# Scan features read in place by TensorE instead of being moved into one tile per group

## The chip, the core and the metric

The kernel runs on one core of a Trainium2 chip. Its time is the device time of one execution, in microseconds (us). Three runs of the kernel before gave 675.22, 677.21 and 671.78 us, a median of 675.22. The execution that was profiled took 673.33 us, with a span of 671.6 us.

## The reference

The reference has three parts that follow each other. A gated linear scan runs for 4 batches and 8 heads over 768 steps, with a complex decay per step and per feature:

```
S_re, S_im = ar*S_re - ai*S_im + k[t] (x) v[t],  ar*S_im + ai*S_re     # 48 x 48 per head
y[t] = q[t] @ S_re
```

Its outputs, 3072 tokens of 8 x 48 = 384 numbers, go through a mixture of eight experts (tokens with a positive skip score are routed to the expert with the largest logit, relu(x w1) w2, added to x), and then through a second mixture (normalised tokens against normalised expert vectors, every token routed). Everything is float32.

## The kernel before, in words

**Features.** The scan is computed in closed form. The cumulative sums of log magnitude and of phase are taken along time (`front` and `back` in `feat`), and q and k are multiplied by the growth and decay factors and by cosine and sine of the phase. A score between two steps is then a plain dot product over 96 features of a head: 48 "real" products (times cosine) and 48 "imaginary" ones (times sine). The work is cut into 8 groups g (4 batches, two halves of 384 steps); group 0 and group 7 are cut once more in time (`PARTS`). In a group, 384 features of the 8 heads lie on 3 blocks of 128 partitions. VectorE (DVE) writes the real products into tile PR (one buffer) and the imaginary ones over QK (three buffers); both are made at line 536.

**The move.** The 128 partitions of PR and QK don't hold a head's 96 features together. Line 548 moves them by DMA into ST (two buffers), where each head has rows 0 to 95: five transfers per part from PR on SP's queue, five from QK on POOL's queue. `PIECES` lists them, `head` and `row` say where they land.

**Chunks.** A group has 3 chunks of 128 steps, 24 in all (k). For a chunk, TensorE (PE) does the following, with ScalarE (ACT) and DVE emptying PSUM:

- W, line 601: 8 matmuls of 96 rows, one a head, k-features against q-features, into PS0 and PS1 (`half(0)` and `half(1)`); DVE multiplies by the causal mask into WM (line 604).
- K, line 612: 8 transposes of the k-features into PS2 and PS3, copied by ACT to KT (line 615); not for the last chunk of a batch.
- y, line 628: 8 matmuls WM x V and, from the second chunk of a batch on, 8 matmuls with the running state SS, in pairs: the even head's 48 output columns go to PSUM partitions 0 to 47, the odd head's to 64 to 111, all in PS4.
- U, line 637: 8 matmuls KT x V that add to the state in PS5, copied by ACT to SS (line 641); not for the last chunk of a batch.
- x, line 648: 4 matmuls that bring y to token order with the first router's logits; ACT copies the token rows (line 651) and they are stored; DVE reduces the logits (line 654).

After the last chunk the routing is finished, and the two mixtures of experts (lines 938 to 1284) run on PE.

**What sets the order.** All instructions are collected in a list by `Plan`, each with an engine, a cost in us, what it reads and writes, and a due time; `Plan.order` sorts them in a list schedule, forwards and backwards several times, and keeps the shortest. Each engine then executes its own list strictly in that order. Where the planner sees PE idle, `run` inserts filler matmuls (`warm`, line 438) with no use but to keep PE busy. So a change of a cost or of a dependence moves instructions on every engine.

Of the kernel before, what the change touches and what calls it, by code (L numbers as in the profile page):

```python
# [41 lines left out]
FILL = 0.6  # L42
PARTS = {0: ((0, 1), (1, 3)), 7: ((0, 2), (2, 3))}
# [235 lines left out]
def kernel(  # L279
# [132 lines left out]
    NRI, NQK = 4, 3  # L412
    ST = [st_p.tile([P, 2 * H * TS], F32, name=f"ST{i}") for i in range(2)]
    SS = [st_p.tile([96, H, 64], F32, name=f"SS{i}") for i in range(2)]
    WM = [[st_p.tile([P, 4, P], F32, name=f"WM{i}{j}") for j in range(2)] for i in range(2)]
    KT = [[st_p.tile([P, 4, 96], F32, name=f"KT{i}{j}") for j in range(2)] for i in range(2)]
# [4 lines left out]
    QK = [el.tile([P, 2 * NB * TS], F32, name=f"QK{i}") for i in range(NQK)]  # L421
    T1 = [el.tile([P, NB * TS], F32, name=f"T1{i}") for i in range(2)]
    T2 = [el.tile([P, NB * TS], F32, name=f"T2{i}") for i in range(2)]
    PR = el.tile([P, 2 * NB * TS], F32, name="PR")
# [5 lines left out]
    nc.vector.memset(PS[4], 0.0)  # L430
    nc.gpsimd.memset(SQ2, 1.0)
# [8 lines left out]
    def feat(g):  # L440
# [26 lines left out]
        k1, k2, kp = (lambda j: K("t1", g % 2, j)), (lambda j: K("t2", g % 2, j)), (lambda j: K("pr", 0, j))  # L467
# [45 lines left out]
        def back(i, j):  # L513
# [26 lines left out]
            vp = part(PR, 2 * NB, j)  # L540
            dve(2 * n, lambda: mul(vp, vre), kre(j) + kqk(j), kp(j))
            dve(2 * n, lambda: mul(vc, vim), kim(j), kqk(j))
            d = part(ST[g % 2], 2 * H, j)
            for x, ks, a0 in ((vp, kp, 0), (vc, kqk, 1)):
                for y, (h, bk, p0, o, m) in enumerate(PIECES):
                    nh = h[1] - h[0]
                    eng, add, us = (nc.gpsimd, pool, 1.0) if a0 and g in POOLST else (nc.sync, dma, 0.64)
                    add(MOVE * wide(j) / P * nh * m / D, lambda x=x, a0=a0, h=h, nh=nh, bk=bk, p0=p0, o=o, m=m, eng=eng: eng.dma_start(  # L548
                        d[row(h, a0) + o : row(h, a0) + o + m, 2 * h[0] * w : 2 * h[1] * w],
                        x[p0 : p0 + m, 2 * bk * w : 2 * (bk + nh) * w]),  # L550
                        ks(j), [("st", g % 2, y, a0, i) for i in range(j.start, j.stop)], cost=us)

        def run(part):
            plan.bias = LEAD
# [17 lines left out]
    def kst(g, hs, cs):  # L572
        return [("st", g % 2, y, a, i) for y, (h, *_) in enumerate(PIECES)
                if any(h[0] <= x < h[1] for x in hs) for a in range(2) for i in cs]
# [6 lines left out]
    def chunk(k):  # L581
# [3 lines left out]

        def st(z, h):
            o = (2 * H * s0 + head(z, h) * (s1 - s0) + c - s0) * P
            return ST[g % 2][0:96, o : o + P]

# [5 lines left out]
        def half(hh):  # L595
            hs = range(4 * hh, 4 * hh + 4)
            wt = PS[hh][:, 0:512].rearrange("p (h t) -> p h t", h=4)

            def w_():
                for h in hs:  # L600
                    nc.tensor.matmul(wt[:, h % 4, :], lhsT=st(1, h), rhs=st(0, h), start=True, stop=True)  # L601

            pe(0.95, w_, kst(g, hs, [c]), [("ps", hh)], D0 - 4)
            dve(512, lambda: nc.vector.tensor_tensor(  # L604
                WM[k % 2][hh], wt, maskT.rearrange("p (o t) -> p o t", o=1).to_broadcast([P, 4, P]), op=ALU.mult),
                [("ps", hh), "mask"], [("wm", k % 2, hh)], D0 - 2)
            if not last:
                kt = PS[2 + hh][:, 0:384].rearrange("p (h t) -> p h t", h=4)

                def k_():  # L610
                    for h in hs:
                        nc.tensor.transpose(kt[:, h % 4, :], st(1, h), ident[0:96, 0:96])

                pe(0.35, k_, kst(g, hs, [c]), [("ps", 2 + hh)], D0 - 3)
                act(384, lambda: nc.scalar.copy(KT[k % 2][hh], kt), [("ps", 2 + hh)], [("kt", k % 2, hh)], D0 - 1)

        for hh in range(2):
            half(hh)
# [3 lines left out]
        def y_():  # L622
            for p in range(NPR):
                for x in range(2 if i else 1):
                    for j in range(2):
                        h = 2 * p + j
                        w, r = (so[:, h, 0:D], st(0, h)) if x else (vt[:, c, h, :], WM[k % 2][h // 4][:, h % 4, :])
                        nc.tensor.matmul(py[64 * j : 64 * j + D, p, :], lhsT=w, rhs=r, start=(x == 0), stop=(x == 1 or i == 0))  # L628

        pe(1.8 if i else 0.95, y_, [("wm", k % 2, 0), ("wm", k % 2, 1), ("v", g % 2)] + kst(g, range(H), [c])  # L630
           + ([("S", k % 2)] if i else []), [("ps", 4)], D0)
        if not last:
            pu = PS[5][0:96, 0:DM].rearrange("d (h e) -> d h e", h=H)

            def u_():
                for h in range(H):
                    nc.tensor.matmul(
                        pu[:, h, :], lhsT=KT[k % 2][h // 4][:, h % 4, :], rhs=vt[:, c, h, :], start=not i and not h, stop=True, skip_group_check=True)

            pe(1.48, u_, [("kt", k % 2, 0), ("kt", k % 2, 1), ("v", g % 2)], [("ps", 5)], D0 + 1)  # L640
            act(DM, lambda: nc.scalar.copy(sn[:, :, 0:D], pu), [("ps", 5)], [("S", (k + 1) % 2)], D0 + 3)
# [202 lines left out]
    pe(0.5, lambda: nc.tensor.matmul(PS[7][:, 384:512], lhsT=PR[:, 0:P], rhs=ident, start=True, stop=True), [("pr", 0, 0)], [], -100.0)  # L844
# [27 lines left out]
    def make_l():  # L872
# [751 lines left out]
```

## Time and profile before

| | |
|---|---|
| median of three runs | 675.22 us (671.78 to 677.21) |
| the profiled execution | 673.33 us, span 671.6 us |
| PE busy | 606.9 us, 90% of the span |
| DVE busy | 462.1 us, 69% |
| ACT busy | 411.1 us, 61% |
| POOL busy | 187.2 us, 28% |
| DMA | 116.39 MB |

Shares over the whole span mix three stages: the start, in which PE has nothing to do; the scan with its 24 chunks; and the experts. The rows further down are cut by stage. Between two rows of a timeline the difference of their start times says how long the first one held its engine; the duration beside it includes the latency of the last instruction.

### The profile page before, as it was taken

The page shows a single profiled execution, that of the slowest core. Times are in us where ns is not written, and L with a number is a line of the kernel's source. Part 1 is how long each engine was busy: PE and PEld are TensorE (multiplying, and loading weights), DVE is VectorE, ACT ScalarE, POOL GpSimd, SP SyncE. Part 2 cuts the span into 40 slices and gives each one's busy share as a digit, 9 for nine tenths or more (in the row PEclk, how much of TensorE's full clock was granted, in tenths as well). Part 3 has the DMA queues.
Part 4 walks back from the last instruction along what each step waited for, and adds up shares of the span by engine and source line. Part 5 has one row for each costly group of instructions (what it writes and reads, how often), then busy time and mean ns, then how long its engine had stood idle before and what let it go on. Part 6 is the DMA issues. An engine that isn't in the chain of part 4 may idle for free. (4 is left out here: it accounts for less than half of the span.)

```text
span 671.6 us, 12986 instructions
## 1 busy us (share of the span) xinstructions
PE 606.9 (90%) x4764; PEld 581.9 (87%) x4764; DVE 462.1 (69%) x1035; ACT 411.1 (61%) x735; POOL 187.2 (28%) x233
## 2 busy tenths in 40 slices
PE   0179699998999999999999999999999999999993
PEld 0178699987989988999999999989998989999993
DVE  4999699998996465767776657778466474655340
ACT  5997869787887453755555545166467474664430
POOL 5112011014634433223443133233141313213111
PEclk9997889999999999999999999999999999999998
DMA  8748999889476677766644430474325434355101
GB/s 317 277 120 208 202 246 303 239 205 267 114 186 155 227 256 227 252 228 219 194 172 132 129 113 20 113 282 146 118 73 184 153 122 144 129 189 176 47 11 36
DMA packets 39079, 116.39 MB, mean 173 GB/s; under 512 B 8573, under 2 KB 14275, under 8 KB 36322
## 3 DMA queue, kind: packets, MB, share of 16 engines
q1 hardware_dynamic: 28354, 84.97, 40.0%
q0 software_dynamic: 10656, 30.53, 16.4%
q8 instruction: 39, 0.64, 0.4%
q14 instruction: 30, 0.25, 0.1%
HBM read 83.78 MB, written 14.09 MB: 146 GB/s over the span
## 5 line engine op out<-in xcount | busy, mean ns | idle before, releaser
L969 PE MATMUL PS<-x,w 128*128 128x256 f32 (+4 forms) x1152 | 179.3, 313 | 1.1 <-DVE h L982 0.6
L1019 PE MATMUL PS<-w,h 128*128 128x384 f32 x968 | 179.4, 340 | 0.4 <-ACT xA L1278 0.4
L969 PEld LDWEIGHTS PS<-x,w 128*128 128x128 f32 x1152 | 171.4, 190 | 2.7 <-DVE x L945 0.7
L1019 PEld LDWEIGHTS PS<-w,h 128*128 128x128 f32 x968 | 166.1, 189 | 2.2 <-ACT xA L1278 1.7
L975 ACT ACTIVATE h<-PS 128x256 fp32r<-128x256 f32 (+4 forms) x136 | 57.4, 422 | 103.7 <-PE PS L969 103.5
L982 DVE SCALAR_TENSOR_TENSOR h<-PS,h 128x256 fp32r<-128x256 f32 (+3 forms) x152 | 64.7, 436 | 71.3 <-ACT h L975 43.0
L1284 POOL DMA_INDIRECT out<-o,ts2i x30 | 30.9, 1029 | 164.0 <-ACT o L1274 108.9
L919 DVE TENSOR_TENSOR w<-r,w 128x768 fp32r<-128x768 f32 x64 | 59.3, 952 | 8.0 <-ACT w L918 4.4
L913 DVE TENSOR_TENSOR w<-r,w 128x1024 fp32r<-128x1024 f32 x45 | 53.9, 1223 | 11.1 <-ACT w L912 9.9
L601 PE MATMUL PS<-ST 96*128 96x128 f32 x384 | 54.5, 289 | 7.1 <-DVE WM L604 2.9
L601 PEld LDWEIGHTS PS<-ST 96*128 96x128 f32 x384 | 48.4, 199 | 10.1 <-DVE WM L604 3.8
L918 ACT CAST w<-r 128x768 fp32r<-128x768 f32 x64 | 51.7, 834 | 8.9 <-PE PS L1019 6.1
L438 PE MATMUL PS<-cst 128*128 128x128 f32 x332 | 49.2, 295 | 3.3 <-DVE w8s L731 2.2
L912 ACT CAST w<-r 128x1024 fp32r<-128x1024 f32 x45 | 45.7, 1049 | 7.4 <-DMA r<-in_w1b 7.0
L438 PEld LDWEIGHTS PS<-cst 128*128 128x128 f32 x332 | 44.6, 207 | 4.3 <-DVE w8s L731 2.6
L548 POOL DMA_DIRECT2D ST<-QK x50 | 25.6, 524 | 80.7 <-DVE QK L536 37.0
L604 DVE TENSOR_TENSOR WM<-PS,cst 128x512 f32<-128x512 f32 x48 | 32.4, 680 | 14.5 <-PE PS L601 14.4
L944 ACT CAST x<-PS 128x256 fp32r<-128x256 f32 (+4 forms) x48 | 19.8, 426 | 32.4 <-PE PS L938 31.8
L1086 POOL DMA_INDIRECT xd<-o,ts1i x16 | 17.0, 1061 | 78.9 <-DVE o L1083 37.9
L740 POOL DMA_INDIRECT tab<-LG,ixa x24 | 28.7, 1195 | 32.0 <-DMA ts1f<-tab 8.2
L628 PE MATMUL PS<-WM,VT 128*48 128x128 f32 x384 | 37.2, 282 | 0.1
L1032 POOL DMA_INDIRECT xg<-xd,ts2i x30 | 32.0, 1067 | 13.5 <-issue 5.3
(217 smaller groups left out, 982.5 us busy)
## 6 DMA issues: line engine op xcount, KB each, us to landing
r<-in_w1a SPq DMA_DIRECT2D x24, 512.0 KB, 5.7
r<-in_w2a SPq DMA_DIRECT2D x32, 384.0 KB, 3.8
r<-in_w1b SPq DMA_DIRECT2D x24, 512.0 KB, 3.9
r<-in_w2b SPq DMA_DIRECT2D x32, 384.0 KB, 5.4
RI<-in_ri SPq DMA_DIRECT2D x6, 1152.0 KB
QK<-in_qk SPq DMA_DIRECT2D x6, 1152.0 KB, 18.1
ST<-PR SPq DMA_DIRECT2D x12, 432.0 KB, 6.2
ST<-QK POOLq DMA_DIRECT2D x12, 432.0 KB, 10.1
```

Source lines behind the costliest of these rows:

```text
L438: nc.tensor.matmul(PS[7][:, 384:512], lhsT=ident, rhs=ident, start=True, stop=True)
L601: nc.tensor.matmul(wt[:, h % 4, :], lhsT=st(1, h), rhs=st(0, h), start=True, stop=True)
L604: dve(512, lambda: nc.vector.tensor_tensor(WM[k % 2][hh], wt, maskT.rearrange("p (o t) -> p o t", o=1).to_broadcast([P, 4, P]), op=ALU.mul ...
L628: nc.tensor.matmul(py[64 * j : 64 * j + D, p, :], lhsT=w, rhs=r, start=(x == 0), stop=(x == 1 or i == 0))
L912: act(F, lambda s=s: nc.scalar.copy(T["w1"][q % 2][0][s], T["r1"][q % 2][s]), [("r1", q % 2, j), "L"], [k + (0,)])
L913: dve(F, lambda s=s: nc.vector.tensor_tensor(T["w1"][q % 2][1][s], T["r1"][q % 2][s], T["w1"][q % 2][0][s].bitcast(F32), op=ALU.subtract), ...
L918: act(2 * DM, lambda s=s: nc.scalar.copy(T["w2"][0][s], T["r2"][s]), [("r2", j)], [k + (0,)])
L919: dve(2 * DM, lambda s=s: nc.vector.tensor_tensor(T["w2"][1][s], T["r2"][s], T["w2"][0][s].bitcast(F32), op=ALU.subtract), [("r2", j), k + ...
L969: nc.tensor.matmul(ph, lhsT=l, rhs=r, start=(i == 0), stop=(i == len(seq) - 1))
L975: act(wa, lambda f=f, ph=ph: nc.scalar.activation(T[name][:, f, o0 : o0 + wa], ph[:, 0:wa], AF.Relu), [("ps", f % 3), "w" if name == "hA" ...
L982: dve(b - a, lambda f=f, ph=ph, a=a, b=b, o=o: nc.vector.scalar_tensor_tensor(T[name][:, f, o : o + b - a], ph[:, a - c0 : b - c0], 0.0, T ...
L1019: nc.tensor.matmul(po if n == P else po[0 : 2 * stride], lhsT=x, rhs=w[:, f, :], start=(f == 0 and i == 0), stop=(f == NF - 1 and i == len ...
```

## The change

The features are laid out so that heads 0 to 5 lie two to a block, each on 48 partitions that start at 0 or at 64, and PE reads them where DVE wrote them: 48 rows of real products in PR, 48 of imaginary ones in QK, so that a head's dot product is two matmuls of 48 rows added in PSUM. An even head uses the partitions from 0, an odd head those from 64 (two row groups of the array). Heads 6 and 7 fill the gaps (16 rows in each of three blocks) and are still moved to ST, which now holds these two heads alone: six transfers per part from PR and six from QK, of 16 partitions each. PR gets three buffers, QK four. W, K, y and U are rewritten for this; WM and KT are now kept by even and odd heads or by real and imaginary products. PS5 is cleared at the start, and group 0 is given an earlier due time (`LEADS`). The planner's costs for W, K, y and U are named numbers.

```
-PIECES = [((0, 3), 0, 0, 0, 48), ((3, 6), 0, 48, 0, 48), ((6, 8), 0, 96, 0, 32), ...]
+LEADS = {0: -40.0}
+COST_W, COST_K, COST_Y, COST_U = 1.95, 0.36, 2.4, 1.45
+PIECES = [((h, h + 1), h // 2, 64 * (h % 2), 0, 48) for h in range(6)]
+MOVED = [((h, h + 1), b, 48 + 64 * (h - 6), 16 * b, 16) for h in (6, 7) for b in range(NB)]
+PIECES += MOVED
...
-    NRI, NQK = 4, 3
-    ST = [st_p.tile([P, 2 * H * TS], F32, name=f"ST{i}") for i in range(2)]
+    NRI, NQK, NPB = 4, 4, 3
+    ST = [st_p.tile([P, 4 * TS], F32, name=f"ST{i}") for i in range(2)]
...
+    nc.vector.memset(PS[5][:, 0:DM], 0.0)
...
-            pe(0.95, w_, kst(g, hs, [c]), [("ps", hh)], D0 - 4)          # twice, one for 4 heads
+        def w_():
+            for b in range(NB):
+                for a in range(2):
+                    for j in range(2):
+                        nc.tensor.matmul(wt[j][:, b, :], lhsT=xf(1, a, b)[rows(j)], rhs=xf(0, a, b)[rows(j)], start=(a == 0), stop=(a == 1))
+            for j in range(2):
+                nc.tensor.matmul(wt[j][:, NB, :], lhsT=st(1, 6 + j), rhs=st(0, 6 + j), start=True, stop=True)
+        pe(COST_W, w_, sum(kf, []), [("ps", 0), ("ps", 1)], D0 - 4)
...
+                def k_(hh=hh, kt=kt):
+                    for b in range(NB):
+                        nc.tensor.transpose(kt[:, 2 * b : 2 * b + 2, :].rearrange("p h t -> p (h t)"), xf(1, hh, b), ident)
+                    nc.tensor.transpose(kt[:, 6:8, 0:D], st(1, 6 + hh), ident[0:96, 0:96])
...
+            for h in range(H):
+                mm(h, vt[:, c, h, :], WM[k % 2][h % 2][:, h // 2, :], h < 2, not i)
+            if i:
+                for h in (6, 7):
+                    mm(h, so[0:96, h, 0:D], st(0, h), False, True)
+                for b in range(NB):
+                    for a in range(2):
+                        for j in range(2):
+                            mm(2 * b + j, so[rows(j), 2 * b + a, 0:D], xf(0, a, b)[rows(j)], False, a == 1)
...
+                for b in range(NB):
+                    for a in range(2):
+                        for j in range(2):
+                            nc.tensor.matmul(
+                                pu[rows(j), 2 * b + a, :], lhsT=KT[k % 2][a][:, 2 * b + j, :], rhs=vt[:, c, 2 * b + j, :],
+                                start=not i and not a and not b, stop=True, skip_group_check=True)
```

The order of instructions, at three places. In these rows L601 and L606 are W (the L608 rows its last two matmuls), L612 and L620/L621 are K, L628 and L631 are y, L637 and L652/L656 are U, L648 and L668 are x, L438 and L433 are fillers; the numbers behind a tile's name tell its buffer.

First, PE at y of the second chunk of a batch. Before:

```order
L628 MATMUL PS4_101<-WM10_111,VT0_117 48x128 x2
L628 MATMUL PS4_101<-ST0_105,SS1_108 48x128 x2
L628 MATMUL PS4_101<-WM10_111,VT0_117 48x128 x2
L628 MATMUL PS4_101<-ST0_105,SS1_108 48x128 x2
L628 MATMUL PS4_101<-WM11_112,VT0_117 48x128 x2
L628 MATMUL PS4_101<-ST0_105,SS1_108 48x128 x2
```

With the change, the end of the same step and the start of the next chunk's W:

```order
L631 MATMUL PS4_101<-ST0_105,SS1_108 48x128 x2
L631 MATMUL PS4_101<-PR0_135,SS1_108 48x128 x2
L631 MATMUL PS4_101<-QK0_127,SS1_108 48x128 x2
L631 MATMUL PS4_101<-PR0_135,SS1_108 48x128 x2
L631 MATMUL PS4_101<-QK0_127,SS1_108 48x128 x2
L631 MATMUL PS4_101<-PR0_135,SS1_108 48x128 x2
L631 MATMUL PS4_101<-QK0_127,SS1_108 48x128 x2
L606 MATMUL PS0_97<-PR0_135 128x128
L606 MATMUL PS1_98<-PR0_135 128x128
L606 MATMUL PS0_97<-QK0_127 128x128
L606 MATMUL PS1_98<-QK0_127 128x128
```

The state part of y was four pairs that read ST; it is now one pair from ST and six pairs that read PR and QK, and W alternates between the two row groups and between two PSUM banks.

Second, SP's queue at the move of group 2 (the third group). Before:

```order
L653 DMA xd_63<-XT0_119 128x384
L548 DMA ST0_105<-PR_134 48x2304 x2
L548 DMA ST0_105<-PR_134 32x1536
L548 DMA ST0_105<-PR_134 16x768 x2
L653 DMA xd_63<-XT1_120 128x384
```

With the change:

```order
L673 DMA xd_63<-XT0_119 128x384
L465 DMA RI1_124<-in_ri 128x2304
L542 DMA ST0_105<-PR2_137 16x768 x6
L673 DMA xd_63<-XT1_120 128x384
L673 DMA xd_63<-XT0_119 128x384
```

Two transfers of 48 partitions, one of 32 and two of 16 have become six of 16 partitions, and a load of a later group's input stands ahead of them.

Third, PE where the seventh chunk (the first of group 2) begins. Before:

```order
L628 MATMUL PS4_101<-ST1_106,SS0_107 48x128 x2
L648 MATMUL PS6_103<-lane_73,XTT1_122 128x113 x4
L601 MATMUL PS0_97<-ST0_105 128x128 x4
L628 MATMUL PS4_101<-WM10_111,VT1_118 48x128 x2
L628 MATMUL PS4_101<-ST1_106,SS1_108 48x128 x2
```

With the change:

```order
L631 MATMUL PS4_101<-QK1_128,SS1_108 48x128 x2
L433 MATMUL PS7_104<-cst_66 128x128 x4
L668 MATMUL PS6_103<-lane_73,XTT1_122 128x113 x4
L433 MATMUL PS7_104<-cst_66 128x128 x15
L606 MATMUL PS0_97<-PR2_137 128x128
L606 MATMUL PS1_98<-PR2_137 128x128
```

Before, W of the seventh chunk comes ahead of y of the sixth. Now the six chunks of the first batch are done with x and all, 19 fillers stand there, and from here to the end of the scan the order holds 2 more fillers (20 stood behind this place before).

## Rows read from the trace of the kernel before

**Rows 1.** Four stages: length, busy us (x instructions) of each engine, granted clock, DMA share, GB/s.

```profile
39.80:104.93 65.13, 53.60 (x497) 50.82 (x495) 57.13 (x72) 53.16 (x62) 8.01 (x16) 0.84 0.81 196
104.93:237.00 132.07, 125.23 (x1434) 117.85 (x1432) 111.99 (x205) 103.54 (x152) 44.49 (x57) 1.00 0.78 212
237.00:244.70 7.70, 6.46 (x54) 5.87 (x53) 5.50 (x39) 3.74 (x8) 1.10 (x1) 1.00 0.75 221
244.70:671.60 426.90, 412.12 (x2721) 397.83 (x2719) 257.25 (x669) 219.34 (x477) 122.28 (x131) 0.99 0.44 146
```

**Rows 2.** The fillers (L438) alone, third stage: length, PE busy, PEld busy.

```profile
104.93:237.00 132.07, 6.47 (x41) 5.26 (x41) 1.00 0.78 212
```

**Rows 3.** Waits of PE in the third stage: us, times, longest us.

```profile
PE PS L601 <- DVE WM L604: 2.2, 2, 1.7
PE PS L648 <- DVE LG L654: 2.0, 2, 1.2
```

**Rows 4.** Timeline of DVE: start, us, instruction, idle before it.

```profile
60.76 2.53 DVE L536 TENSOR_TENSOR QK<-QK,RI 128x2304 f32<-128x2304 f32 x1
...
83.11 0.69 DVE L604 TENSOR_TENSOR WM<-PS,cst 128x512 f32<-128x512 f32 x1 [5.33 <-PE PS L601]
83.72 1.01 DVE L478 TENSOR_TENSOR_SCAN T<-T,lend,lmt 128x384 f32<-128x384 f32 x1
84.64 2.53 DVE L536 TENSOR_TENSOR PR<-QK,RI 128x2304 f32<-128x2304 f32 x1
...
87.21 2.56 DVE L536 TENSOR_TENSOR QK<-QK,RI 128x2304 f32<-128x2304 f32 x1
...
212.98 0.96 DVE L536 TENSOR_TENSOR QK<-QK,RI 128x768 f32<-128x768 f32 x1
```

**Rows 5.** Timeline of PE: first product, fourth chunk, seventh chunk's W.

```profile
30.29 0.80 PE L844 MATMUL PS<-cst,PR 128*128 128x128 f32 x2 [30.29 <-DVE PR L536]
...
82.27 0.80 PE L601 MATMUL PS<-ST 96*128 96x128 f32 x2 [2.10 <-DMA ST<-QK]
...
104.93 1.07 PE L601 MATMUL PS<-ST 96*128 96x128 f32 x8
```

**Rows 6.** Moves issued up to 104.93 us: count, KB each, median us to landing.

```profile
ST<-QK POOLq DMA_DIRECT2D x4, 432.0 KB, 16.5
```

**Rows 7.** Small moves, up to 240 us: count, KB each, median us to landing.

```profile
ST<-PR SPq DMA_DIRECT2D x4, 16.0 KB, 2.3
ST<-QK POOLq DMA_DIRECT2D x4, 16.0 KB, 3.8
```

**Rows 8.** Timeline of SP: one load that is now issued before the features' inputs.

```profile
5.03 0.92 SPq L798 DMA_DIRECT2D lane<-in_wr  x1
```

**Rows 9.** Timeline of PE in the middle of the scan, at full granted clock.

```profile
132.22 2.04 PE L601 MATMUL PS<-ST 96*128 96x128 f32 x16
134.09 0.49 PE L612 MATMUL PS<-cst,ST 96*128 96x96 f32 x4
134.51 0.43 PE L628 MATMUL PS<-WM,VT 128*48 128x128 f32 x4
134.77 0.39 PE L628 MATMUL PS<-ST,SS 96*48 96x128 f32 x4
...
136.09 0.39 PE L628 MATMUL PS<-ST,SS 96*48 96x128 f32 x4
136.41 1.16 PE L601 MATMUL PS<-ST 96*128 96x128 f32 x8
137.41 1.48 PE L637 MATMUL PS<-VT,KT 128*96 128x48 f32 x16
138.73 1.11 PE L648 MATMUL PS<-lane,XTT 128*128 128x113 f32 x8
```

**Rows 10.** Timeline of PE: three transposes of 128 x 128 in the experts.

```profile
290.30 0.49 PE L1095 MATMUL PS<-cst,o 128*128 128x128 f32 x3
290.54 3.48 PE L969 MATMUL PS<-x,w 128*128 128x256 f32 x27
```

More of the change, by code (lines that the diff above doesn't have):

```diff
@@ L420 @@
     RI = [el.tile([P, 2 * NB * TS], F32, name=f"RI{i}") for i in range(NRI)]
-    QK = [el.tile([P, 2 * NB * TS], F32, name=f"QK{i}") for i in range(NQK)]
+    QK = [(el if i < 2 else st_p).tile([P, 2 * NB * TS], F32, name=f"QK{i}") for i in range(NQK)]
     T1 = [el.tile([P, NB * TS], F32, name=f"T1{i}") for i in range(2)]
     T2 = [el.tile([P, NB * TS], F32, name=f"T2{i}") for i in range(2)]
-    PR = el.tile([P, 2 * NB * TS], F32, name="PR")
+    PR = [(el if i == 2 else st_p).tile([P, 2 * NB * TS], F32, name=f"PR{i}") for i in range(NPB)]
     onet = el.tile([P, TS], F32, name="onet")
@@ L538, in mul @@
                     x.rearrange("p (j k t) -> p j k t", k=1, t=w).to_broadcast([P, NB, 2, w]), op=ALU.mult)
-            vp = part(PR, 2 * NB, j)
+            vp = part(PR[g % NPB], 2 * NB, j)
             dve(2 * n, lambda: mul(vp, vre), kre(j) + kqk(j), kp(j))
             dve(2 * n, lambda: mul(vc, vim), kim(j), kqk(j))
-            d = part(ST[g % 2], 2 * H, j)
+            d = part(ST[g % 2], 4, j)
             for x, ks, a0 in ((vp, kp, 0), (vc, kqk, 1)):
[L545 to L550, printed above, removed]
+                for y, ((h, _), bk, p0, o, m) in enumerate(MOVED):
+                    eng, add, us = (nc.gpsimd, pool, 0.6) if a0 and g in POOLST else (nc.sync, dma, 0.64)
+                    add(MOVE * wide(j) / P * m / D, lambda x=x, a0=a0, h=h, bk=bk, p0=p0, o=o, m=m, eng=eng: eng.dma_start(
+                        d[a0 * D + o : a0 * D + o + m, 2 * (h - 6) * w : 2 * (h - 5) * w],
+                        x[p0 : p0 + m, 2 * bk * w : 2 * (bk + 1) * w]),
                         ks(j), [("st", g % 2, y, a0, i) for i in range(j.start, j.stop)], cost=us)
         def run(part):
-            plan.bias = LEAD
+            plan.bias = LEADS.get(g, 0.0)
             for i, j in enumerate(bl):
@@ L584, in chunk, with xf, rows @@
         s0, s1 = next(x for x in cells(g) if x[0] <= c < x[1])
+        X = PR[g % NPB], QK[g % NQK]
+        kf = kst(g, range(s0, s1)), [("pr", g % NPB, x) for x in range(s0, s1)], [("qk", g % NQK, x) for x in range(s0, s1)]
         def st(z, h):
[L587 removed]
+            o = (4 * s0 + (2 * (h - 6) + z) * (s1 - s0) + c - s0) * P
             return ST[g % 2][0:96, o : o + P]
+        def xf(z, a, b):
+            o = (2 * NB * s0 + (2 * b + z) * (s1 - s0) + c - s0) * P
+            return X[a][:, o : o + P]
+        def rows(h):
+            return slice(64 * (h % 2), 64 * (h % 2) + D)
         D0 = T0 + STEP * k
@@ L593, in chunk @@
         last = i == NTB - 1
[L595 to L601, printed above, removed]
-            pe(0.95, w_, kst(g, hs, [c]), [("ps", hh)], D0 - 4)
-            dve(512, lambda: nc.vector.tensor_tensor(
-                WM[k % 2][hh], wt, maskT.rearrange("p (o t) -> p o t", o=1).to_broadcast([P, 4, P]), op=ALU.mult),
+        wt = [PS[hh][:, 0:512].rearrange("p (h t) -> p h t", h=4) for hh in range(2)]
@@ L622, in y_, with mm @@
         def y_():
[L623 to L630, printed above, removed]
+            def mm(h, l, r, start, stop):
+                j = h % 2
+                nc.tensor.matmul(py[64 * j : 64 * j + D, h // 2, :], lhsT=l, rhs=r, start=start, stop=stop, skip_group_check=True)
```

50 lines of the change are left out of this document (22 added, 28 removed).

## The prediction

> **What bounds the kernel now.** I read the stages first. Behind 244.7 us PE works 412.1 us of 426.9 at full granted clock [rows 1], on experts that the change doesn't touch: it can only move the point at which they begin. That point hangs on the scan's last y, whose rows end at 237.0; 7.7 us of routing follow. In the stretch from 104.93 (W of the seventh chunk, [rows 5]) to 237.0, PE is busy 125.2 us of 132.1, DVE 112.0, ACT 103.5 [rows 1]; 6.5 us of PE's busy time are fillers [rows 2]. So PE's slack there is 6.8 idle + 6.5 fillers = 13.3 us of 132, or 10%. What idle there is ends on hand-overs from DVE (2.2 us for WM, 2.0 for LG, [rows 3]), of one or two microseconds each. **PE is the bound of these 18 chunks, with DVE and ACT close behind.** This can also be read from DVE: its last feature product ends at 213.9 [rows 4], 23 us before the last y. PE has a backlog of some three chunks by then.
>
> Before 104.93 it is different. PE has nothing but fillers until the first features exist (30.29 us idle, [rows 5]), and from 39.8 to 104.93 it is busy 53.6 of 65.1 us at a granted clock of 0.84 on average [rows 1]. There the move hurts: the second group's QK product ends at 63.3 [rows 4], and PE waits for its move until 82.27 [rows 5], 19 us later; 432 KB pieces issued in this part took 16.5 us to land [rows 6]. DVE in turn idled 5.33 us for that W [rows 4].
>
> **The change, part by part.** All matmuls are float32, and each shows as two records in the timeline. Prices are differences of start times in one stretch at full clock [rows 9].
>
> W: 16 records, 8 matmuls, take 134.09 - 132.22 = 1.87 us, 0.234 each. The trace before shows no two matmuls in different row groups. It shows pairs in different column groups: y's rows are 0.22 apart for a pair ((136.09 - 134.77) / 6), so a pair costs about what one matmul does. Bounds for a row-group pair: 0.22 (side by side) and 0.47 (one after the other); nothing makes a pair cheaper than one. I take 0.22, since the y pair is the nearest row. Six pairs and two full matmuls: 1.32 + 0.47 = 1.79.
>
> Changes of array shape: y's 8 pairs take 136.41 - 134.51 = 1.90, of which 8 x 0.22 = 1.76; so entering and leaving paired form costs 0.14, or 0.07 a change. W gains two changes: 1.79 + 0.14 - 1.87 = **+0.06 a chunk**; upper bound with 0.47 a pair +1.6.
>
> y: four state pairs become one from ST and six of 48 rows; that is three pairs more and one change of shape more: 0.66 + 0.07 = **+0.73**, where there is a state (15 of the 18 chunks). Upper bound, if the six pairs don't overlap: 1.5 more.
>
> U: 8 matmuls take 138.73 - 137.41 = 1.32, 0.165 each; now six column pairs and two single ones. With a pair at the price of one matmul it is 8 x 0.165 again; two changes of shape add 0.14. If narrower weights make a pair cheaper (y's pair halves at 0.11), it is 0.33 less; if pairs don't overlap, 1.0 more. I take **+0.14** (15 chunks).
>
> K: 8 transposes again, six of them 128 wide; three such take 290.54 - 290.30 = 0.24 [rows 10], 0.08 each, against (134.51 - 134.09) / 4 = 0.1 with a change of shape [rows 9]. **0.** x and all of DVE's and ACT's work per chunk are the same.
>
> Sum for the stretch: 18 x 0.06 + 15 x 0.73 + 15 x 0.14 = 1.1 + 11.0 + 2.1 = **+14.2 us of PE**. Against it stands the slack. The order now holds 2 fillers in place of 20 here, 10% of 6.5 us, so 5.8 come back; of the 6.8 idle I let 6 vanish, since an engine that falls behind finds its inputs ready. **-11.8.** If the hand-overs stay as they are, it is only -5.8.
>
> The stretch also **begins earlier**. W of the seventh chunk needs group 2. Its QK product ended at 89.8 (87.21 + 2.56); the 5.33 us of DVE's wait before it go, because W of the fourth chunk needs a quarter of the bytes moved. But by the new order this product stands behind 5 more masks (0.61 each, from 83.11 to 83.72), 3 more scans (0.92, from 83.72 to 84.64) and one more pass over 1152 elements (half a product, 1.3): +7.1. The start is later too: SP now issues three small loads, one of them 0.92 us long [rows 8], ahead of the features' inputs, and the expert norms come first on ACT and DVE; about +1.5. So QK is done at 89.8 - 5.3 + 7.1 + 1.5 = 93.1. The move stays, but six issues of 16 partitions on POOL at about 0.5 us, 3.1, and a landing between 2.3 (small moves, [rows 7]) and 16.5 [rows 6]; small pieces are nearest, I take 3.8. That gives 100.0 (98.5 to 113) in place of 104.93: **-4.9.** The queue past which the move goes: SP has a load of RI ahead of it that must wait for its buffer; by the order its last reader is far earlier, so I cost it at nothing. If it is late, W is late by as much.
>
> Before 100 PE does the first six chunks, 0.9 us more each, in a stretch where it is idle 11.5 us [rows 1]: nothing, as long as the features of group 2 are later than PE. POOL's and SP's twenty extra issues (some 10 us over the scan) lie on engines that wait for features. The DMA saves three quarters of the moved bytes; that has been counted as landing time and in DVE's wait. Clearing PS5 (0.4 us of DVE in its idle start): nothing.
>
> Sum: -4.9 + 14.2 - 11.8 = **-2.5 us** on the profiled execution's 673.3 us, **671**. The median of the runs shown is 1.9 above that execution, so the same on the median's footing is 673.
>
> **Rivals.**
>
> *A larger gain.* The new order waits for PE nowhere on DVE, and PE is kept warm through the first batch, where the clock before was 0.84. If moved pieces land in 2.3, the start's 1.5 doesn't arise, DVE's own idle before its products shrinks, and U's pairs come at the cheap end (-0.47 x 15 = -7), the end moves by some 12 to 14: **660**. For it: DVE and ACT have 20 and 28 us free in the stretch [rows 1]. Against it: PE's added work is sure, and the features' order puts masks first.
>
> *Slower, by y's pairs.* In y the two row groups write the same PSUM tile PS4, at partitions 0 and 64; in W they write PS0 and PS1. If two row groups can't write one bank at once, y's six pairs cost 0.47 in place of 0.22: +1.5 x 15 = +22.5, and the result is **693**. It decides from 0.03 a pair on, where my gain is used up (0.1 is 1% slower). Against it: column pairs in y share this very bank today at 0.22 a pair [rows 9]. That is a bank shared by column groups, though, not by row groups. The Trainium skill, TensorEngine Tiling (Array Packing), section Gotcha 1: PSUM Pressure, says that different row tiles write different banks and can't access the same bank simultaneously; by that rule it would be this rival, and no row here shows two row tiles at all.
>
> *Slower, by W's loads.* Every pair in W loads two sets of 128 columns. If these loads queue, W's matmuls keep 0.234 each: 6 x 0.25 = +1.5 a chunk, x 18 = +27, **697**; with y's as well 720. Against it: in the row-wise form the two weights sit in separate rows. For it: U's matmuls at 48 columns cost 0.165, far above half of W's 0.234 at 128, so something other than columns streamed has a price there [rows 9].
>
> *No gain at all.* Features are late (DVE has no slack in the first 100 us), the seventh chunk starts at 105 and the idle of hand-overs stays: -0 + 14.2 - 13 to -9: 674 to **678**.
>
> **Chances.** Forecast (664 to 676) 0.50; larger gain 0.18; no gain 0.13; y's pairs 0.10; W's loads 0.06, both 0.03. The result counts as changed from about 1%, 6.7 us, which is near the spread of the runs. Faster by more: the larger gain and the forecast's lower third, 0.18 + 0.19 = 0.37. Slower: 0.19 and a little of the no gain, 0.21. Within: 0.42. Range: from 657 (larger gain with every bound) to 693 (y's pairs): it leaves out the dearer half of the slow cases and little else, 0.12. The forecast's own range is 664 to 676.
>
> **What would show it.** In the timeline of PE: W's alternating rows at 0.22 a pair (right) or 0.47; y's six state pairs at 0.22 or 0.47; y's whole step at 2.6 where it was 1.9. The seventh chunk's W at 98 to 102. In the stretch behind it fillers under 1 us and PE idle under 2; the last y's end within 230 to 239. The moves' landing under 6 us, and no wait of W for ST over 2 us. Wrong it would be if PE were idle 5 us or more there (then DVE or ACT has become the bound), or if the experts' 427 us changed by more than 2: I let them stand as they are.

## The result, and the profile after

The changed kernel takes 680.0 us in the median of 20 runs (675.6 to 687.0), the kernel before 673.7 in 20 runs beside it. The ratio is 1.0088, with a 95% interval of 1.0061 to 1.0115: **6 us slower**, where 2.5 us faster had been forecast. The profiled execution took 681.34 us with a span of 679.4, so 8 us more than that of before; the accounts below are made between these two. Executions of one kernel lie as far apart, so such an account holds for this pair and not to the tenth for the kernels. Ratios leave out executions over 1.5% above the fastest of their kernel (here one of each); the traces of e1 and e12 are of such executions.

The stages of the profile after, cut at the same points as [rows 1] (W of the seventh chunk, end of the last y, first expert): length, busy us (x instructions) of PE, PEld, DVE, ACT and POOL, granted clock, DMA share, GB/s.

```profile
36.53:103.54 67.01, 61.47 (x732) 55.28 (x731) 61.31 (x77) 57.91 (x68) 9.75 (x20) 0.90 0.46 147
103.54:241.00 137.46, 133.30 (x1925) 119.39 (x1924) 115.72 (x210) 103.18 (x151) 49.39 (x63) 0.99 0.48 144
241.00:245.86 4.86, 3.66 (x30) 3.12 (x29) 2.80 (x22) 1.76 (x5) 1.00 (x1) 1.00 0.38 108
245.86:679.40 433.54, 415.06 (x2725) 400.09 (x2723) 256.89 (x671) 219.03 (x476) 121.28 (x130) 0.99 0.44 144
```

DMA fell from a share of 0.78 to 0.48 in the scan. PE's busy time in the second stage rose from 125.2 to 133.3, and of that time only 0.88 is fillers where it was 6.47 [rows 2]; idle fell from 6.8 to 4.2. The waits of PE that are left between 103.54 and 241.04:

```profile
PE PS L620 <- ACT KT L624: 2.3, 2, 2.0
PE PS L606 <- DVE WM L612: 1.1, 1, 1.1
PE PS L608 <- DMA ST<-QK: 0.7, 1, 0.7
```

The wait for moved features is 0.7 us. A chunk on PE, at full clock, as in [rows 9] (L606 and L608 are W, L631 y, L652 and L656 U, L668 x, L620 and L621 K):

```profile
175.99 0.74 PE L652 MATMUL PS<-VT,KT 128*48 128x48 f32 x24
176.66 0.54 PE L656 MATMUL PS<-VT,KT 128*96 128x48 f32 x4
177.13 0.49 PE L606 MATMUL PS<-PR 48*128 48x128 f32 x4
177.45 0.39 PE L606 MATMUL PS<-QK 48*128 48x128 f32 x4
177.68 0.39 PE L606 MATMUL PS<-PR 48*128 48x128 f32 x4
...
178.67 0.71 PE L608 MATMUL PS<-ST 96*128 96x128 f32 x4
179.31 1.08 PE L631 MATMUL PS<-WM,VT 128*48 128x128 f32 x16
180.22 0.39 PE L631 MATMUL PS<-ST,SS 96*48 96x128 f32 x4
180.54 0.42 PE L631 MATMUL PS<-PR,SS 48*48 48x128 f32 x4
180.80 0.39 PE L631 MATMUL PS<-QK,SS 48*48 48x128 f32 x4
181.01 0.39 PE L631 MATMUL PS<-PR,SS 48*48 48x128 f32 x4
...
181.99 1.15 PE L668 MATMUL PS<-lane,XTT 128*128 128x113 f32 x8
182.97 0.49 PE L620 MATMUL PS<-cst,PR 128*128 128x128 f32 x3
...
183.89 0.49 PE L606 MATMUL PS<-PR 48*128 48x128 f32 x4
```

Four records are one pair (two matmuls of two records), and the rows are 0.22 apart, in W and in y: **the row groups run side by side**, also in y, where both write PS4. W takes 179.31 - 177.13 = 2.18 us, y 2.68, U 1.14, K 0.92 for its 8 transposes.

The seventh chunk's W, to be held against [rows 5], and what PE did before it:

```profile
97.75 1.16 PE L433 MATMUL PS<-cst 128*128 128x128 f32 x8
99.10 1.15 PE L668 MATMUL PS<-lane,XTT 128*128 128x113 f32 x8 [0.20 <-ACT XTT L663]
100.08 3.53 PE L433 MATMUL PS<-cst 128*128 128x128 f32 x30
103.54 0.49 PE L606 MATMUL PS<-PR 48*128 48x128 f32 x4
```

L433 are fillers: PE had finished six chunks and had nothing to do until the third group's features came. DVE made them later than forecast ([rows 4] has their times before), and waited for PE three times on the way (2.26, 2.59 and 0.61 us):

```profile
50.88 0.23 DVE L674 TENSOR_REDUCE LG<-PS 128x17 f32<-128x68 f32 x1 [2.26 <-PE PS L668]
...
70.78 1.29 DVE L612 TENSOR_TENSOR WM<-PS,cst 128x512 f32<-128x512 f32 x2 [2.59 <-PE PS L608]
...
90.39 2.55 DVE L531 TENSOR_TENSOR PR<-QK,RI 128x2304 f32<-128x2304 f32 x1
92.86 0.68 DVE L612 TENSOR_TENSOR WM<-PS,cst 128x512 f32<-128x512 f32 x1
93.46 2.55 DVE L531 TENSOR_TENSOR QK<-QK,RI 128x2304 f32<-128x2304 f32 x1
```

### The profile page after: what moved, and what is told of

It is laid out like the page before. It is cut to its first block, busy times and chain, and to the rows that moved or that the text cites. A ratio compares the mean times of both kernels' runs of the same rounds, so it can differ in the third digit from the quotient of the medians.

```text
span 679.4 us, 14653 instructions
## 1 busy us (share of the span) xinstructions
PE 637.9 (94%) x5584; PEld 601.9 (89%) x5584; DVE 464.6 (68%) x1036; ACT 412.6 (61%) x736; POOL 193.2 (28%) x243
## 4 chain that ended last, share of the span: by engine, by line
PE 58%; issue 12%; DMA 9%; ACT 8%; DVE 8%; POOL 2%; SPq 1%; POOLq 0%; DVEq 0%; ACTq 0%
PE PS L989 18%; PE PS L1039 16%; PE PS L631 7%; PE PS L606 4%; DMA out<-o,ts2i 3%; DMA r<-in_w1b 3%; PE PS L668 2%; ACT L375 2%; PE PS L958 2%; PE PS L608 2%; PE PS L652 2%; PE PS L620 1%; DMA tab<-LG,ixa 1%; PE PS L1123 1%; PE PS L656 1%
## 5 line engine op out<-in xcount | busy, mean ns | idle before, releaser
L542 POOL DMA_DIRECT2D ST<-QK x60 | 29.6, 503 | 120.7 <-DVE QK L531 63.1
L433 PE MATMUL PS<-cst 128*128 128x128 f32 x384 | 53.2, 292 | 1.3 <-DVE cs L845 0.9
L433 PEld LDWEIGHTS PS<-cst 128*128 128x128 f32 x384 | 49.8, 206 | 2.6 <-DVE cs L845 0.9
L760 POOL DMA_INDIRECT tab<-LG,ixa x24 | 30.6, 1275 | 33.4 <-DMA LE<-tab 8.9
L612 DVE TENSOR_TENSOR WM<-PS,cst 128x512 f32<-128x512 f32 x48 | 31.0, 680 | 8.2 <-PE PS L608 8.0
L965 DVE TENSOR_TENSOR x<-PS,x 128x256 fp32r<-128x256 f32 (+4 forms) x48 | 22.3, 484 | 18.7 <-ACT x L964 18.4
L1052 POOL DMA_INDIRECT xg<-xd,ts2i x30 | 31.1, 1038 | 11.1 <-issue 5.3
L606 PE MATMUL PS<-PR 48*128 48x128 f32 x288 | 31.3, 289 | 1.2 <-DVE WM L612 1.1
```

Source lines behind the costliest of these rows:

```text
L433: nc.tensor.matmul(PS[7][:, 384:512], lhsT=ident, rhs=ident, start=True, stop=True)
L606: nc.tensor.matmul(wt[j][:, b, :], lhsT=xf(1, a, b)[rows(j)], rhs=xf(0, a, b)[rows(j)], start=(a == 0), stop=(a == 1))
```

## The experiments

Ratios are to the kernel before, with 95% intervals; the changed kernel's own is 1.0088. Four theories were tried one after the other. **P**: PE's added work sets the time. **O** and **S**: the order that the planner makes decides; a cost changed by a little gives another order of the same instructions and scatters the end. **Q**: one place in the order decides, the third group's QK product on DVE. F, E, K and M stand explained in the expectations.

### PE's work in an unchanged order

*e1_y3.* In the changed kernel's y, state part:

```
-for a in range(2):
-    for j in range(2):
-        mm(2 * b + j, so[rows(j), 2 * b + a, 0:D], xf(0, a, b)[rows(j)], False, a == 1)
+for j in range(2):
+    mm(2 * b + j, so[rows(j), 2 * b, 0:D], xf(0, 0, b)[rows(j)], False, True)
```

> The changed kernel without the imaginary half of the state term of heads 0 to 5: y's last six pairs become three (order and everything else the same). Theory P (matmul work of the 18 chunks behind the seventh chunk's W sets when the experts begin): 3 pairs x 0.22 us = 0.66 us less a chunk, 15 chunks with a state in that stretch, -9.9 us; the time falls from 681 to about 671, the last y's end from 241.0 to about 231, and PE's idle time and fillers in the stretch stay as small as they are. Theory F (the features, their order on DVE, set it): PE turns the freed time into idle time, the end moves by 0 to -3 us, 678 to 681. Theory E (part of the loss arises in the routing and the experts): even when the last y's end falls, the time from it to the end stays about 4 us longer than before.

0.9999 (0.9964 to 1.0035): 6 us less than the change, for 13.2 us of matmuls taken out (20 chunks with a state). The profiled execution took 681.8 us where the median is 673.8, so only its scan is read. There most of the gain lies in the first six chunks. The QK product of the third group and W of the seventh chunk:

```profile
67.09 1.29 DVE L612 TENSOR_TENSOR WM<-PS,cst 128x512 f32<-128x512 f32 x2 [0.79 <-PE PS L608]
...
89.07 2.54 DVE L531 TENSOR_TENSOR QK<-QK,RI 128x2304 f32<-128x2304 f32 x1
```

```profile
99.15 0.49 PE L606 MATMUL PS<-PR 48*128 48x128 f32 x4
```

Both are 4.4 us earlier, for 5 x 0.66 = 3.3 us of matmuls at full clock. Behind that W the other 9.9 us brought only 1.7 (the stage takes 135.8 us in place of 137.5): PE's idle time there rose from 4.2 to 7.7 us, and the granted clock fell to 0.96 on average, as this row shows.

```profile
99.15:234.98 135.83, 128.16 (x1745) 112.73 (x1744) 115.49 (x210) 103.04 (x151) 49.67 (x63) 0.96 0.50 148
```

This execution has the lowest mean clock of the twelve (0.969), so the 0.96 and with it the 1.7 us may be its own. P holds for the first batch, where I had costed the added work at nothing; that F holds for most of the rest is read from this one trace and not shown.

*e2_pe09.* In the kernel before, at the end of y: `+            warm(4)`

> The kernel before, with four idle matmuls of 128 columns (0.22 us each, the fillers' form) at the end of every chunk's y: the change's added matmul time alone, 0.9 us a chunk, with the old moves and the old order. Theory P: 18 x 0.9 = 16 us against 13.3 us of fillers and idle time, of which some 11 are given up: +3 to +6 us, 677 to 680 on the profiled execution's footing of 673.3. If the slack cannot be given up: +16, 690. Theory F (the loss is in the order of the features): 0 to +2, 673 to 675.

1.0266 (1.0214 to 1.0319): 15 us between the medians, 18 by the ratio, near the sum in which no slack is given up. The stage from the seventh W on (it begins at 107.56; the row is cut at 107.00):

```profile
107.00:248.96 141.96, 140.77 (x1583) 134.65 (x1581) 112.59 (x205) 104.23 (x152) 48.89 (x57) 1.00 0.72 194
```

The last y ends 12 us later than in [rows 1], of which 2.6 arose before the seventh W; the rest of the 15 came in the experts. The stage takes 141.4 us, 9.3 more than before, for 15.8 us of added matmuls. PE's idle time fell from 6.8 to 1.2 us, so idle time does come back in this order, as forecast; the fillers, which the forecast also counted as slack, stayed where they were.

*e6_nofill.* In the kernel before, no fillers between the W steps of the seventh and the last chunk (`+        if 6 in seen and NK - 1 not in seen: return` in `warm`, `seen` holding the chunks whose W has been given out).

> The kernel before without the fillers from the seventh chunk's W to the last chunk's W (19 rows of filler matmuls, about 6 us of PE); order the same. The forecast let 5.8 us of them come back as slack. If fillers stand where PE would otherwise work: -4 to -6, 667 to 669. If PE is idle in their place (it waits for hand-overs there): -1 to 0, 672 to 673. If TensorE's granted clock falls where they stood: slower, 674 or above.

1.0021 (0.9981 to 1.0061): no gain. In this row PE works nearly as long as with the fillers and the clock is lower, 0.96 in place of 1.00:

```profile
104.70:238.51 133.81, 126.00 (x1394) 117.61 (x1393) 112.15 (x201) 103.36 (x152) 48.64 (x57) 0.96 0.77 211
```

**Fillers are not slack here**: without them the other matmuls take their 6 us at a lower granted clock.

### Transfers, and what waits behind them

*e3_traffic.* In the changed kernel, behind each third move:

```
+if y % 3 == 2:
+    r = y // 3
+    eng.dma_start(junk[g][a0, r, :, 6 * P * j.start : 6 * P * j.stop], x[64 * r : 64 * r + 48])
```

> The changed kernel with the bytes that it no longer moves copied all the same, from the same products at the same points of the same queues, into a scratch in DRAM that nobody reads. If the saved traffic is worth something (loads of features and weights that land sooner): 3 us or more slower than the change, 684 or above. If nobody waited for it (theory P: matmul work sets the time): 0 to +1.5 us, 680 to 683.

1.0636 (1.0586 to 1.0686). It doesn't price the traffic alone, as I had meant: the copies share SP's queue with the storing of x. ACT waited for its buffer of x, and PE then for ACT:

```profile
ACT XT L679 <- DMA xd<-XT: 11.8, 2, 11.0
```

```profile
PE PS L628 <- ACT KT L632: 17.9, 3, 12.0
```

What the saved bytes are worth without that wait stays open.

*e4_ucol.* In the kernel before, U as 16 products of 48 columns in pairs. For this the second half of a head's features moves to rows 64 to 111 of ST, so W, K and y's state part read 112 rows, 16 of them empty (the steps took 1.89, 0.83 and 1.86 us, against 1.87, 0.84 and 1.90 before):

```
-pu[:, h, :], lhsT=KT[k % 2][h // 4][:, h % 4, :], rhs=vt[:, c, h, :], ...
+for a in range(2):
+    pu[64 * a : 64 * a + D, h, :], lhsT=KT[k % 2][h // 4][:, h % 4, a * D : a * D + D], rhs=vt[:, c, h, :], ...
...
-pe(1.48, u_, ...
+pe(1.2, u_, ...
```

> The kernel before, with moved features for all heads, but U in column pairs: 16 products of 48 columns, the real half to partitions 0 to 47, the imaginary to 64 to 111. In the changed kernel such pairs took 0.112 us each, so U falls from 1.32 us to some 0.9 to 1.0 with the changes of shape. Theory P: 0.3 to 0.4 us less a chunk x 18 = -5 to -7 us of matmul work; PE has idle time already, so half of it shows: 669 to 671 where before is 673. Theory F: 0, 673 to 674. Against it: the column-pair form loads two sets of 48 columns for each pair; if that costs 0.165 a product, U takes 2.6 us and it is +20, 690.

1.0412 (1.0361 to 1.0463), though U does take 0.82 us:

```profile
150.28 0.89 PE L641 MATMUL PS<-VT,KT 128*48 128x48 f32 x32
151.10 0.99 PE L615 MATMUL PS<-cst,ST 112*128 112x112 f32 x8
```

The lower planned cost gave another order, in which stores of x stand on SP's queue behind moves that wait for DVE (36 to 245 us, first ACT's waits, then those of SP's queue):

```profile
ACT XT L656 <- DMA xd<-XT: 22.6, 5, 8.0
...
SPq L551 <- DVE PR L539: 52.6, 8, 13.5
```

Besides, 4.2 us were lost at the start: GpSimd cleared ST's empty rows ahead of a constant that the scans need, which came at 12.45 us in place of 1.78.

*e5_ucol_kept.* The same in the order of before, with that clearing later:

```
-pe(1.2, u_, ...
+pe(1.48, u_, ...
-    for t in ST: nc.gpsimd.memset(t[32:64], 0.0)
-pool(0.0, lambda: nc.gpsimd.memset(zr, 0.0), ...
+pool(0.0, lambda: [nc.gpsimd.memset(t, 0.0) for t in [zr] + [x[32:64] for x in ST]], ...
```

> The kernel before with U in column pairs again, but in before's own order on every engine (U's planned cost is left at 1.48, and the clearing of the 16 empty rows of ST stands on GpSimd behind the constants). In e4_ucol U took 0.82 us in place of 1.32, yet the kernel was 25 us slower, and ACT waited 22.6 us for rows of x to be stored. Theory P (matmul work sets the time): 0.5 us less a chunk x 20 = -10 us of work, of which e1_y3 and e2_pe09 let two thirds to nine tenths through: -6 to -9, 664 to 667. Theory O (e4_ucol lost by its order alone): the wait for the stored rows is gone, 673 or less. Theory K (the copies of KT or the pairs themselves cost): still 690 or more.

1.0264 (1.0206 to 1.0323). ACT's wait for stored rows fell from 22.6 to 4.0 us. Theory O is right that part of e4's loss was its order (10 us lie between the two by their ratios, of which 1.5 are the clearing), and wrong that 673 would be reached; P's gain didn't come. The time lies in K's range, 690 or more, but the copies of KT take 480 ns where they took 479, and U is shorter, so K's cause is not seen. 2.7 us are lost in the first features, by a mishap of my edit that is told in the last section. Why the rest is slower is open; 8.6 us of it come behind the last y (443.1 us to the end in place of 434.5). Up to 250 us PE waits 8.5 us for moved features, where it waited 2.1 before:

```profile
PE PS L602 <- DMA ST<-QK: 8.5, 4, 5.4
```

### The same instructions in other orders

All of these change numbers that the planner reads, and no instruction's form or count but for fillers.

```
 change       LEADS = {0: -40.0}             COST_W, COST_K, COST_Y, COST_U = 1.95, 0.36, 2.4, 1.45
 e7_lead0     LEADS = {}
 e8_costs                                    2.18, 0.46, 2.68, 1.14
 e9_nudge                                    2.0, 0.36, 2.4, 1.45
 e10_raised                                  2.18, 0.46, 2.68, 1.45
 e11_u_only                                  1.95, 0.36, 2.4, 1.14
 e13_group2_early  {0: -40.0, 2: -4.0}       1.95, 0.36, 2.4, 1.45
 e14_group2_late   {0: -40.0, 2: 12.0}       2.18, 0.46, 2.68, 1.45
 e16_best          {0: -40.0, 2: -4.0}       2.18, 0.46, 2.68, 1.45
 before       W 0.95 a half, K 0.35, y 1.8, U 1.48
 e12_before_costs  W 0.935, K 0.42, y 1.90, U 1.32
 e15_before_nudge  W 0.975
 e17_before_k36    K 0.36
 e18_before_y185   y 1.85
```

> The changed kernel without the bias of -40 for the first group's second half (the planner orders anew). Theory P: the same work per chunk, another start: the seventh chunk's W within 3 us of 103.5, the end within 4 us of 680. Theory O (small differences of order decide as much as the work does): more than 5 us either way.

> The changed kernel, planned with the matmul costs that its trace shows (W 2.18, K 0.46, y 2.68, U 1.14 us; before 1.95, 0.36, 2.4, 1.45). The instructions are the same, the order is another. Theory P: -2 to +1 us, 678 to 681, since PE's work is the same. Theory O: more than 5 us either way.

> The changed kernel with W's planned cost at 2.0 in place of 1.95 us and nothing else: the same instructions in another order, with costs that are no nearer to the trace as a set. Theory M (e8_costs is 10 us faster because its planned costs are the measured ones): 677 to 683, like the change. Theory S (the planner's order is sensitive, any nudge of a cost scatters the end): more than 4 us away from 680 in either direction, and then the change's +6 us is in part the luck of one order.

> The changed kernel with three planned costs raised to the measured ones (W 2.18, K 0.46, y 2.68), U left at 1.45 (measured 1.14). Theory M: most of e8_costs' 10 us come from the costs that were too low, so 670 to 675. If it is U's, 678 to 682. Theory S: anywhere from 668 to 685.

> The changed kernel with U's planned cost lowered to the measured 1.14, the other three left. Theory M: little, 676 to 682. Theory S: anywhere from 668 to 685.

> The kernel before, planned with the matmul costs that its own trace shows (W 0.935 a half, K 0.42, y 1.90, U 1.32; before 0.95, 0.35, 1.8, 1.48). Theory M: a gain here too, since costs were off by 5 to 20%: 667 to 672. If the gain of e8_costs belongs to the change (features read in place can start earlier when they are planned rightly): 672 to 676. Theory S: anywhere from 666 to 690.

| order | ratio to before (95%) | median us | seventh W | last y ends | from there to the end |
|---|---|---|---|---|---|
| change | 1.0088 (1.0061 to 1.0115) | 680.0 | 103.5 | 241.0 | 438.4 |
| e7_lead0 | 1.0107 (1.0048 to 1.0166) | 681.0 | 103.3 | 239.0 | 440.2 |
| e11_u_only | 1.0073 (1.0042 to 1.0103) | 676.3 | 100.8 | 238.7 | 439.3 |
| e9_nudge | 1.0038 (1.0011 to 1.0065) | 674.4 | 95.6 | 236.0 | 437.1 |
| e8_costs | 0.9944 (0.9911 to 0.9977) | 670.1 | 95.7 | 232.6 | 435.2 |
| e10_raised | 0.9944 (0.9917 to 0.9970) | 669.1 | 93.9 | 233.8 | 433.6 |
| before | 1 | 673.7 | 104.9 | 237.1 | 434.5 |
| e12_before_costs | 1.0216 (1.0166 to 1.0267) | 688.4 | 103.6 | 254.9 | 434.6 |

(The last three columns are from one profiled execution each.) e7 stayed where P had put it (103.3 and 681.0). **e8 and e10 beat the kernel before by 0.6% and the change by 1.4%**, with the changed kernel's instructions. In e8's trace W of the seventh chunk follows on y with no filler between:

```profile
95.40 0.39 PE L631 MATMUL PS<-QK,SS 48*48 48x128 f32 x4
95.71 0.49 PE L606 MATMUL PS<-PR 48*128 48x128 f32 x4
```

It comes 7.8 us earlier than in the change, and the last y ends 8.4 earlier; the stage between is as long as it was:

```profile
95.71:232.60 136.89, 135.42 (x1946) 120.94 (x1944) 120.69 (x224) 107.92 (x156) 50.07 (x63) 1.00 0.50 152
```

M, that planned costs help by being the measured ones, agrees with e10 and e11 in the main but is not it: a nudge to 2.0 of one cost (measured 2.18) already takes off 0.5%, and measured costs in the kernel before add 14 us. S is left, or Q, since DVE began the third group's QK product at 86.5 to 87.0 us in e8, e9 and e10, at 90.4 in e11, and at 93.5 and 93.7 in the change and e7. Four more runs tell these apart.

> The changed kernel with a bias of -4 us on the third group's features, so that VectorE reaches their QK product behind 8 masks in place of 12 (some 6 us of its work less ahead). Theory Q (the start of that product sets the seventh chunk and with it the end): the product starts at 86 to 88 in place of 93.5, the seventh chunk's W by 98, the end at 670 to 676. Theory P (matmul work alone sets the end): 678 to 682. Theory S (order scatters without one cause): anywhere from 668 to 685.

> e10_raised, the best order so far (669.1), with a bias of +12 us on the third group's features: 12 masks ahead of their QK product, as in the changed kernel. Theory Q: the product starts some 3 to 6 us later than the 86.5 of e10_raised, and the end moves up by as much, 672 to 676. Theory P: 668 to 671. Theory S: anywhere from 666 to 685.

> The kernel before with W's planned cost at 0.975 us a half in place of 0.95: the same instructions in another order. If the order that it has is a lucky one among many: 676 to 690, as e12_before_costs (688) was. If orders of the kernel before lie close together: 671 to 676. Theory Q (product at 66.7 us of VectorE's work, near the 65.6 of before): 672 to 676.

> e10_raised with a bias of -4 us on the third group's features: 8 masks ahead of their QK product in place of 10, some 7 us of VectorE's work less. Theory Q: the product starts at 80 to 84, the seventh chunk's W before 95; if PE can take it up, 664 to 668; if PE is the bound by then (it still has the first six chunks to do), no gain, 668 to 670. Theory S: anywhere from 666 to 685.

e13: 1.0136 (1.0089 to 1.0183). The product came even earlier than asked, the seventh W at 98.0, and nothing was gained:

```profile
82.80 2.56 DVE L531 TENSOR_TENSOR QK<-QK,RI 128x2304 f32<-128x2304 f32 x1
```

e14: 1.0208 (1.0150 to 1.0267), the product 4.6 us later than in e10, at 91.1, but the end 17 later. e15: 1.0346 (1.0284 to 1.0408), 696 us. e16: 1.0136 (1.0077 to 1.0195), with the product at 77.2 and the seventh W at 91.3, the earliest of all. **Q falls**: an early product was neither enough (e13, e16) nor is it one cause; what is put ahead on DVE puts other work back: in e13 the third chunk's logits are reduced at 89.7 us, in the change at 80.5. That PE's waits for this work are what used up the gain is not shown.

> The kernel before with the planned cost of K at 0.36 in place of 0.35 us: the same instructions in another order. If the order of before is a favourable one among scattered ones (theory S): 676 to 696. If only large changes of the planned costs hurt: 670 to 676.

> The kernel before with the planned cost of y at 1.85 in place of 1.8 us (its trace shows 1.90): the same instructions in another order. Theory S: 676 to 696. If only large changes of the planned costs hurt: 670 to 676.

e17: 1.0016 (0.9967 to 1.0065). e18: 1.0114 (1.0017 to 1.0212). So with e12 and e15 four other orders of the kernel before lie at 1.00, 1.01, 1.02 and 1.03, and none below the one that it has. Nine orders of the changed kernel lie between 0.994 and 1.021. S is what the runs bear out: between orders of one kernel lie 2.6% and 3.5%, more than the largest term of the forecast (14.2 us, 2.1%).

Part of what an order costs is the granted clock. In e15 PE works through nearly as many records from 104.7 us to the last y as in [rows 1], 1426 for 1434, but is busy 134.9 us in place of 125.2, at a clock of 0.93 in place of 1.00, and idle 11.1 in place of 6.8:

```profile
104.70:250.67 145.97, 134.90 (x1426) 126.41 (x1424) 115.94 (x212) 108.74 (x159) 46.22 (x58) 0.93 0.71 197
```

Over all executions the mean granted clock is 0.951 in e15 and 0.963 in e12, where the kernel before beside them has 0.980; it is 0.985 and 0.986 in e8 and e10, 0.978 in the change. (e11, with 0.984 and a ratio of 1.0073, doesn't fit.) Whether the waits of an order lower the clock or something else does, no run separates.

## Why the prediction was wrong

By its own terms, on the profiled executions:

- **Shapes: right in the pairs, W's changes of shape too cheap.** W's and y's pairs cost 0.22 us, and so both slow rivals fall: y's pairs, two row groups, write PS4 at partitions 0 and 64 at the pace of one matmul. By the Trainium skill, TensorEngine Tiling (Array Packing), section Gotcha 1: PSUM Pressure, row tiles can't access one bank at the same time; for two row tiles that write different halves of the partitions the measurement speaks against it. Per chunk W added 0.31 (forecast 0.06), y 0.78 (0.73), U -0.18 (+0.14), K 0.08 (0): 18 x 0.31 + 15 x 0.68 = 15.8 us where 14.2 had been forecast.
- **The start: near in size, by luck.** W of the seventh chunk came 1.4 us earlier, not 4.9. DVE's wait of 5.33 us went, but three others of 5.5 us for PE came, so the QK product ended at 96.0 and not at 93.1. Against that, before, PE still had work of earlier chunks to do behind that point: its stage holds 560 records of y, where 18 chunks have 15 x 32 + 3 x 16 = 528, and 152 of x (the row's 154 counts two that began just before the cut); the stage after holds the 708 of y that 18 chunks have there, and 136 of x. The stage before thus has one y (1.90 us) and two x (0.98 each) more, 3.9 us; at equal content the start gained 5.3. The two rows are y and x in the trace of before:

```profile
104.93:237.00 132.07, 34.83 (x560) 29.71 (x560) 1.00 0.78 212
104.93:237.00 132.07, 20.97 (x154) 18.46 (x152) 1.00 0.78 212
```

- **The stage behind it: the step that failed.** At equal content it grew by 137.5 - 132.1 + 3.9 = 9.3 us, forecast +2.4. PE's busy time without fillers rose by 132.4 - (118.8 - 3.9) = 17.5, where 14.2 stood; half of this difference is the clock, which was 0.57 for 4 us behind a wait of 2 us, the other half W's changes of shape. Of 13.3 us of slack 8.3 came back, not 11.8: the fillers gave 5.6 of 5.8, but of the idle time only 2.7 us went where 6 had been let vanish. "An engine that falls behind finds its inputs ready" is the step that failed. PE's inputs come from DVE and ACT, which wait for PE in turn, and all three are busy 75 to 97% of this stage. It is not so in every order: in e2, in the order of before, 5.6 us of idle time did come back. There 15.8 us of added matmuls lengthened the stage by 9.3, as much as in the change, so added work alone can cost this much. One difference was not tested: W was two steps of four heads, each with its own mask, and is now one step, so the first mask waits for all of it.

```profile
108.87 0.83 PE L620 MATMUL PS<-cst,PR 128*128 128x128 f32 x3 [1.99 <-ACT KT L624]
...
109.00:113.00 4.00, 4.00 (x48) 3.40 (x48) 3.96 (x4) 3.18 (x5) 0.00 (x0) 0.57 0.25 96
```

- **The first six chunks at nothing: wrong.** In e1's trace two thirds of a microsecond a chunk there moved the third group's features by 4.4 us. The masks that DVE makes for these chunks stand ahead of those features in its order, so PE's time is DVE's. That the start came out near all the same is a cancellation.
- **The experts as they stand: not borne out.** From the last y to the end of the span it took 438.4 us in place of 434.5. 2.8 of it arise where the second mixture begins: PE waits 1.79 us for DVE, and the next 45 matmul records take 6.87 us, where before the wait was 0.58 and 45 took 5.24. The granted clock there was 0.75 in place of 1.00. The rows are before's and the change's:

```profile
442.72 5.24 PE L969 MATMUL PS<-x,w 128*128 128x192 f32 x45 [0.58 <-DVE h L982]
...
446.72 6.87 PE L989 MATMUL PS<-x,w 128*128 128x192 f32 x45 [1.79 <-DVE h L1002]
```

In e8 and e10, with the same instructions, the wait is 0.64 and 0.66 and the records take 5.24. Over the profiled orders of the changed kernel the time from the last y lies between 433.6 and 440.3, so I can't put it down to the change.

Start -5.3, stage +9.3, rest +3.8: +7.8, in place of -4.9, +2.4 and 0. Of the rivals, no gain at all (678) came nearest.

Behind these terms stands what the runs showed and the forecast had no place for. **One order was forecast as though it were the change.** The change gave the planner new costs, and the order that came of them is one of many; the others that were run take, by their ratios, 10 us less to 8 us more. The kernel before stands in the best of five orders, with e17 level; the means, 1.0075 over nine orders of the changed kernel and 1.014 over five of before, differ by less than either scatters. The forecast gain of 2.5 us is near what the same instructions gave in e8 and e10 (0.6%, 3.8 us), but nothing in the forecast told these orders from the others, so that is no confirmation. What the change is worth apart from its order can't be told to better than this scatter; that it is slow by itself is not shown, nor that it is fast.

## What to carry to other kernels

Where a scheduler sets the order from a table of costs, an edit that touches a cost is two edits: time a few orders of the same instructions, of the old kernel and of the new, before a difference of 1% is put down to the instructions. Where three engines feed each other in a ring and each is busy for three quarters of the time or more, don't take idle time of the busiest for slack without a run (here 5.6 of 6.8 us came back in one order, 2.7 in another), and don't cost work ahead of a late hand-over at nothing: count from what the late engine has queued before it. When a step is moved to another point of an in-order DMA queue, look at what stands behind it there; a store that frees a buffer can stop two engines.

## What the runs showed of the hardware

- Column pairs of 48 by 48 took 0.112 us each (24 records, 6 pairs, in 0.67 us of U), half of what a pair of 128 streamed columns takes.
- Behind a wait of two to three microseconds PE's granted clock was wholly or mostly at the lower level: after waits of 2.98 us at 43.06 and 2.21 at 61.35, the changed kernel's stretches

```profile
46.00:51.00 5.00, 5.00 (x29) 4.55 (x29) 2.74 (x6) 2.95 (x4) 0.00 (x0) 0.50 0.91 332
...
64.00:69.00 5.00, 5.00 (x51) 4.31 (x52) 4.09 (x4) 2.20 (x4) 1.80 (x4) 0.60 0.37 70
```

  show 0.50 (1.2 GHz) and 0.60, with PE busy all the time. A short wait is thus paid twice, the second time in the work behind it.
- DVE stood still for a clearing on GpSimd. In e5_ucol_kept GpSimd cleared 2 x 32 x 6144 elements from 11.36 to 21.75 us; two copies of 128 x 3 on DVE, which took 0.17 and 0.16 us before, took 3.07 and 3.23, each to the end of one clearing, and the instruction behind each was held until then:

```profile
11.36 10.39 POOL L806 MEMSET ST<- 32x6144 f32 x2
...
13.53 3.07 DVE L482 COPY tend<-RI 128x3 f32<-128x3 f32 x1
14.29 2.31 DVE L507 SCALAR_TENSOR_TENSOR T<-T,T 128x384 f32<-128x384 f32 x1
```

  The Trainium skill, SBUF — State Buffer, section SBUF: two separate sides, says that the two engines share a pair of ports that one of them holds for its whole instruction; the rows agree.
